# Attention in 64-key slots, twelve chunks instead of 22 tiles, in a fused attention and MoE kernel

## The chip, the cores and the metric

One Trainium2 chip, one of its cores. The metric is the device time of one execution in microseconds (us), the median of the runs shown; lower is better. The engines are called as in the profile: PE (TensorE matmul; PEld is its weight load), DVE (VectorE), ACT (ScalarE), POOL (GpSimd) and SP (SyncE, which here only issues DMAs).

## The reference

Strided and local attention over two batches, eight heads, 576 positions, then two expert layers over the 1152 tokens. Heads 0 to 3 see the 32 positions up to their own; heads 4 to 7 see the earlier positions of their own residue modulo 32.

```python
mask_local = (rel >= 0) & (rel < 32)
mask_strided = (rel >= 0) & (pos[None, :] % 32 == pos[:, None] % 32)
scores = np.where(masks, scale * q @ k.T, -1e9)
attn = softmax(scores)                      # the row maximum is taken off first
x = (attn @ v)                              # (1152, 512)
x = ((x @ w1) * (x @ w2)) @ w3 @ w_out      # 512 -> 1024 -> 1024 -> 512
out = sum(p[:, e:e+1] * (np.maximum(x @ e1[e], 0) @ e2[e]) for e in range(4))
```

The scale of q and k makes the scores large, so the softmax needs its maxima.

## The kernel before

The program is written in the order in which each engine shall run its instructions (`tc.manual_schedule`), and each engine runs its own list strictly in that order. It has three parts: attention; the gated product `ab = (x w1) * (x w2)`; and what follows (x3, and the experts in products with split operands).

**Attention** runs in tiles. A tile of the local heads (g = 0) holds 96 queries and up to 128 keys of four heads; a tile of the strided heads (g = 1) holds six or seven residues of 18 positions, 108 or 126 queries against as many keys. A batch has six local and five strided tiles, so there are 22. A tile goes through these methods (class `Tile`): `scores` (L281: one bf16 product of an identity with the mask, then four f32 products, all into one PSUM bank), `maxima` (L291, DVE), `exps` (L298, ACT, four instructions with their sums), `normalise` (L306, DVE), `transposes` (L314, PE), `evac` (L321, half on ACT, half on DVE), `pv` (L325, PE), `put` and `put_lo` (L334, L347: the result split into x_hi on ACT and x_lo on DVE). The loop at L645 is a software pipeline over steps s: in step s the scores of tile s, the normalisation of tile s - 1, the transposes of tile s - 3 and the value products of tile s - 4 are issued.

**Loads.** `load_group` (L241) loads q, k and v of a batch and a group on the SP queue: k as tk, q as two tiles tq with one head of a pair each, the other half zero. All four groups are issued ahead of the loop. q and k of one group are 1.18 MB (576 KB and twice 288 KB). The program gives its DMAs eight semaphores in turn (DMAHW0 to 7), so a DMA waits until the one eight places before has landed.

**Weights.** Class `Chunk` (L109) makes two f32 parts out of a 1 MB load of 64-bit numbers in steps: `round_up` and `magnitude` on ACT, `clamp` (L132), `shift` (L135), `sign` (L138), `add` (L142) on DVE, `split_hi` on ACT, `split_lo` (L159) on DVE. `advance()` (L222) issues the next step, four steps per chunk. There are two raw buffers, so `add` of chunk c is what frees the buffer for the load of chunk c + 2, and `load_next` (L177) issues that load on SP just there.

**The ab units.** `run_unit` (L629) issues one unit of `ab_block` (L353): 24 products of 288 columns, with two steps of the weights. A unit needs x_hi and x_lo of its whole batch and the chunk w12[ft]; two units use one chunk. The loop starts units at step 15 (L644), when all eleven tiles of batch 0 are through, and one unit is issued per step.

Of the kernel before, what the change touches and what calls it, by code (L numbers as in the profile page):

```python
# [18 lines left out]
P = 128  # L19
W = 32  # L20
# [3 lines left out]
RS = [(0, 7), (7, 7), (14, 6), (20, 6), (26, 6)]  # L24
HB = S // 2
# [15 lines left out]
def kernel(  # L41
# [36 lines left out]
    ident_b = const.tile([P, P], BF16, name="ident_b")  # L78
    m_loc = const.tile([P, P], BF16, name="m_loc")
    m_str = const.tile([P, 7, NB], BF16, name="m_str")  # L80

    def constants():
        make_identity(nc, ident_b)
        nc.gpsimd.memset(m_loc, 0.0)

        nc.gpsimd.affine_select(out=m_loc, in_=m_loc, compare_op=ALU.is_ge, fill=NEG,
                                base=W, pattern=[[-1, P]], channel_multiplier=1)
        nc.gpsimd.affine_select(out=m_loc, in_=m_loc, compare_op=ALU.is_ge, fill=NEG,
                                base=-1, pattern=[[1, P]], channel_multiplier=-1)
        make_identity(nc, ident)  # L90
        nc.gpsimd.memset(m_str, 0.0)

        nc.gpsimd.affine_select(out=m_str, in_=m_str, compare_op=ALU.is_ge, fill=NEG,
                                base=0, pattern=[[-NB, 7], [-1, NB]], channel_multiplier=1)
        nc.gpsimd.affine_select(out=m_str, in_=m_str, compare_op=ALU.is_ge, fill=NEG,
                                base=NB - 1, pattern=[[NB, 7], [0, NB]], channel_multiplier=-1)

    def warm_up():

        idle = tmp.tile([P, P], F32, tag="pT", name="idle")  # L100
        nc.vector.memset(idle, 0.0)
# [70 lines left out]
    live = 8  # L172
# [66 lines left out]
    qkv = {}  # L239

    def load_group(b, g, zeros, cut=0):  # L241
# [7 lines left out]
        for c in ([slice(0, cut), slice(cut, S)] if cut else [slice(0, S)]):  # L249
            pairs = slice(2 * g, 2 * g + 2)  # L250
            nc.sync.dma_start(out=tk[:, :, c], in_=kT[b, pairs, :, c].rearrange("k p n -> p k n"))
            for j, r in enumerate(rows):
                queue = nc.scalar if cut and j and c.start == 0 else nc.sync
                queue.dma_start(out=tq[j][r, :, c], in_=qT[b, pairs, r, c].rearrange("k p n -> p k n"))
        vs = []
        src, n = ((v_loc, NL), (v_str, len(RS)))[g]
        for k in range(2):
            tv = wp.tile([P, n, P], F32, tag="w", name="tv")
            nc.sync.dma_start(out=tv, in_=src[b, k])
            vs.append(tv)  # L260
        qkv[b, g] = (tq, tk, vs)

    class Tile:


        def __init__(self, index, b, g, t):
            self.index, self.b, self.g, self.t = index, b, g, t
            self.last = t == (NL, len(RS))[g] - 1
            if g == 0:
                self.nq = QL  # L270
                self.q0 = QL * t
                self.k0 = max(QL * t - W, 0)
                self.nk = QL * (t + 1) - self.k0
                self.mask = m_loc[:QL, P - self.nk:]
            else:
                r0, nr = RS[t]
                self.nq = self.nk = nr * NB
                self.q0 = self.k0 = r0 * NB
                self.mask = flat(m_str)[:self.nq, :self.nk]

        def scores(self):  # L281
            tq, tk, _ = qkv[self.b, self.g]
            nq, nk = self.nq, self.nk
            self.sc = ps_sc.tile([P, 4, P], F32, tag="sc", name="sc")
            mm(self.sc[:nq, :, :nk], ident_b[:nq, :nq], self.mask.unsqueeze(1).to_broadcast([nq, 4, nk]),
               start=True, stop=False)
            for h in range(4):
                mm(self.sc[:nq, h, :nk], tq[h % 2][:, h // 2, self.q0:self.q0 + nq],
                   tk[:, h // 2, self.k0:self.k0 + nk], start=False, stop=h == 3)

        def maxima(self):  # L291
            nq, nk = self.nq, self.nk
            self.neg = small.tile([P, 4], F32, tag="neg", name="neg")
            nc.vector.tensor_reduce(out=self.neg[:nq], in_=self.sc[:nq, :, :nk], axis=mybir.AxisListType.X,
                                    op=ALU.max, negate=True)
            nc.vector.tensor_scalar_mul(self.neg[:nq], self.neg[:nq], SCALE)  # L296

        def exps(self):  # L298
            nq, nk = self.nq, self.nk
            self.p = p_ring[self.index % 4]  # L300
            self.sum = small.tile([P, 4], F32, tag="sum", name="sum")
            for h in range(4):
                nc.scalar.activation(self.p[:nq, h, :nk], self.sc[:nq, h, :nk], AF.Exp,  # L303
                                     bias=self.neg[:nq, h:h + 1], scale=SCALE, accum_out=self.sum[:nq, h:h + 1])

        def normalise(self):  # L306
            nq, nk = self.nq, self.nk
            rec = small.tile([P, 4], F32, tag="rec", name="rec")
# [520 lines left out]
```

## Time and profile before

| | us |
|---|---|
| runs shown | 647.49 (646.29 to 649.39), three runs |
| the profiled execution, its own time | 648.42 |
| its span in the profile | 646.6 |
| PE busy in the span | 629.1 (97%) |
| DVE busy | 470.6 (73%) |
| ACT busy | 291.7 (45%) |

The profiled execution is 0.93 us above the median of the runs, and 1.8 us lie around its span. PE busy counts a pipelined product to its modelled end, so 97% does not say that PE is at its peak. The first two or three slices of 16 us each are the attention; from there on the profile's row of PE stands at nine tenths or more.

### The profile page before, as it was taken

Reading aid. Unit: us, or ns where it says so; the run is one execution under the profiler, and the core shown is the slowest. Engines: PE = TensorE matmul, PEld = TensorE weight load, DVE = VectorE, ACT = ScalarE, POOL = GpSimd, SP = SyncE. Lnnn points to the kernel's source line nnn. Section 1 sums busy time; section 2 is a strip of 40 time slices with the busy share of each in tenths; the row PEclk is TensorE's granted clock in tenths of the full one; section 3 lists DMA queues with packets and bytes.
Section 4 is the critical chain, followed back from the end, with each engine's and each line's share of the span. In section 5 each row is a group of like instructions: output and inputs, shape, how many; then the busy total and the mean of one; then the engine's idle time right before and its main releaser. Section 6 shows DMA issues by size and latency. Waiting matters only on the chain.

```text
span 646.6 us, 10360 instructions
## 1 busy us (share of the span) xinstructions
PE 629.1 (97%) x4052; PEld 572.7 (89%) x4052; DVE 470.6 (73%) x888; ACT 291.7 (45%) x628; POOL 6.9 (1%) x18
## 2 busy tenths in 40 slices
PE   7769999999999999999999999999999999999998
PEld 6659989999888999988999889988788989899896
DVE  8899999599875423777887787787776566665743
ACT  6787776466554323343333343344433333333321
POOL 4000000000000000000000000000000000000000
PEclk9989999999999999999999999999999999999999
DMA  8943133134433310234353355334478474656311
GB/s 227 308 133 131 66 131 131 67 131 143 183 131 130 131 66 1 67 131 188 137 188 138 134 192 183 142 131 163 163 260 322 151 247 153 228 177 239 130 66 66
DMA packets 26385, 98.73 MB, mean 153 GB/s; under 512 B 2528, under 2 KB 3808, under 8 KB 23776
## 3 DMA queue, kind: packets, MB, share of 16 engines
q1 hardware_dynamic: 26192, 97.97, 43.5%
q8 instruction: 32, 0.52, 0.4%
q14 instruction: 17, 0.14, 0.1%
q10 hardware_dynamic: 144, 0.10, 0.1%
HBM read 78.92 MB, written 19.14 MB: 152 GB/s over the span
## 4 chain that ended last, share of the span: by engine, by line
PE 85%; DVE 8%; DMA 3%; ACT 2%; SPq 1%; issue 1%; DVEq 0%
PE g_acc L233 10%; PE g_acc L234 10%; PE g_acc L232 10%; PE ab_acc L232 5%; PE ab_acc L234 4%; PE ab_acc L233 4%; PE m_a L232 4%; PE m_a L234 4%; PE m_a L233 4%; PE x_acc L232 3%; PE x_acc L233 3%; PE x_acc L234 3%; PE m_b L234 3%; PE m_c L232 3%; PE m_c L233 3%; PE m_c L234 3%
## 5 line engine op out<-in xcount | busy, mean ns | idle before, releaser
L517 ACT ACTIVATE h_hi<-u 128x320 fp32r<-128x320 f32 (+1 forms) x128 | 56.9, 445 | 189.2 <-DVE u L523 189.2
L233 PE MATMUL g_acc<-w_lo,h_hi 128*128 128x512 f32 (+1 forms) x296 | 114.9, 388 | 0.0
L232 PE MATMUL g_acc<-w_hi,h_hi 128*128 128x512 f32 (+1 forms) x296 | 114.7, 387 | 0.0
L234 PE MATMUL g_acc<-w_hi,h_lo 128*128 128x512 f32 (+1 forms) x296 | 114.6, 387 | 0.0
L523 DVE TENSOR_TENSOR u<-m_b,u 128x320 f32<-128x320 f32 (+1 forms) x96 | 40.8, 453 | 54.4 <-PE m_b L234 54.4
L456 DVE TENSOR_TENSOR w_lo<-raw,w_hi 128x768 fp32r<-128x768 f32 x64 | 69.4, 1085 | 12.0 <-ACT w_hi L454 11.9
L232 PE MATMUL ab_acc<-x_hi,w_hi 128*128 128x288 f32 x256 | 76.5, 299 | 0.0
L234 PE MATMUL ab_acc<-x_hi,w_lo 128*128 128x288 f32 x256 | 75.4, 295 | 0.0
L233 PE MATMUL ab_acc<-x_lo,w_hi 128*128 128x288 f32 x256 | 75.4, 294 | 0.0
L234 PEld LDWEIGHTS g_acc<-w_hi,h_lo 128*128 128x128 f32 x296 | 55.6, 188 | 12.2
L232 PEld LDWEIGHTS g_acc<-w_hi,h_hi 128*128 128x128 f32 x296 | 55.8, 189 | 8.6
L233 PEld LDWEIGHTS g_acc<-w_lo,h_hi 128*128 128x128 f32 x296 | 55.6, 188 | 8.4
L519 DVE SCALAR_TENSOR_TENSOR h_lo<-u,h_hi 128x320 fp32r<-128x320 f32 (+1 forms) x128 | 57.7, 451 | 3.5 <-ACT h_hi L517 1.4
L454 ACT CAST w_hi<-raw 128x768 fp32r<-128x768 f32 x64 | 59.9, 936 | 0.0
L232 PEld LDWEIGHTS ab_acc<-x_hi,w_hi 128*128 128x128 f32 x256 | 48.0, 187 | 1.5 <-issue 0.3
L233 PEld LDWEIGHTS ab_acc<-x_lo,w_hi 128*128 128x128 f32 x256 | 48.0, 188 | 0.0
L234 PEld LDWEIGHTS ab_acc<-x_hi,w_lo 128*128 128x128 f32 x256 | 48.0, 188 | 0.0
L303 ACT ACTIVATE p_pair<-sc,neg 96x128 f32<-96x128 f32 (+3 forms) x88 | 30.4, 355 | 18.5 <-DVE neg L296 17.3
L233 PE MATMUL m_b<-b_t,s_hi 128*128 128x320 f32 (+1 forms) x128 | 37.8, 295 | 0.0
L523 DVE TENSOR_TENSOR u<-m_a,u 128x320 f32<-128x320 f32 (+1 forms) x64 | 28.9, 452 | 11.8 <-PE m_a L234 11.8
L456 DVE TENSOR_TENSOR s_lo<-raw,s_hi 128x1024 fp32r<-128x1024 f32 x16 | 19.6, 1225 | 23.2 <-ACT s_hi L454 23.2
L121 ACT ACTIVATE raw<-raw 128x1024 int32<-128x1024 uint32 x20 | 23.5, 1174 | 27.4 <-DMA raw<-in_w3T_dram 19.5
(145 smaller groups left out, 1479.4 us busy)
## 6 DMA issues: line engine op xcount, KB each, us to landing
raw<-in_e_dram SPq DMA_DIRECT2D x32, 1024.0 KB, 5.2
raw<-in_w_dram SPq DMA_DIRECT2D x8, 1024.0 KB, 4.9
raw<-in_w3T_dram SPq DMA_DIRECT2D x8, 1024.0 KB, 4.8
stored<-s_hi SPq DMA_DIRECT2D x16, 512.0 KB, 2.6
stored<-s_lo SPq DMA_DIRECT2D x16, 512.0 KB, 2.6
s_hi<-stored SPq DMA_DIRECT2D x16, 512.0 KB, 4.7
s_lo<-stored SPq DMA_DIRECT2D x16, 512.0 KB, 6.2
raw<-in_w_out_dram SPq DMA_DIRECT2D x4, 1024.0 KB, 4.8
```

What stands on the lines that cost most here:

```text
L121: nc.scalar.activation(self.low, self.low.bitcast(U32), AF.Copy, scale=2.0 ** -29)
L232: mm(acc, lh, rh, start=first, stop=False)
L233: mm(acc, lh, rl, start=False, stop=False)
L234: mm(acc, ll, rh, start=False, stop=last)
L303: nc.scalar.activation(self.p[:nq, h, :nk], self.sc[:nq, h, :nk], AF.Exp, bias=self.neg[:nq, h:h + 1], scale=SCALE, accum_out=self.sum[:nq ...
L454: nc.scalar.copy(dst[0], src)
L456: nc.vector.tensor_tensor(out=dst[1], in0=src, in1=dst[0].bitcast(F32), op=ALU.subtract)
L517: nc.scalar.activation(hi, src, AF.Relu)
L519: nc.vector.scalar_tensor_tensor(out=lo, in0=src, scalar=0.0, in1=hi.bitcast(F32), op0=ALU.max, op1=ALU.subtract)
L523: nc.vector.tensor_tensor(out=out, in0=acc, in1=b, op=ALU.add)
```

## The change

The change rewrites the attention (class `Chunk4` for `Tile`), its loads, its place in the loop and the constants.

- A chunk has slots of 64 key columns. Local: six blocks of 32 queries, each against its own 32 keys and the 32 before; the four heads lie in four 32-partition groups of the PSUM bank. So a local chunk has 24 products of 32 queries by 64 keys. Strided: slots of 54 (three residues of 18), two heads side by side in partition halves; 16 products. Six local and six strided chunks, twelve in all.
- The maximum is subtracted on DVE from PSUM into SBUF, the exponential is one ACT instruction in place, the sum is a DVE reduction.
- A chunk is transposed in three (local) or four (strided) products of 128 by 128, evacuated by ACT alone, and multiplied with v in 24 or 16 products of 64 or 54 rows, into two banks.
- The loop has a step less of depth: the transposes come two steps behind the scores and the value products three.
- Loads: the first piece of q and k holds 288 positions (before 192); the value loads are cut up (393 KB per local chunk in one to three DMAs, 0.58 MB for the strided heads of a batch in six); q, k and v of the strided heads of batch 1 are issued after step 7. The second q tile of batch 0 goes by the ACT queue.
- Weight steps: none before step 5, three each in steps 5 to 8 (before: one each in steps 6 to 14). From step 9 on, two units and four weight steps per step.
- Products of zeros without use (`keep_warm`): 14 at the start as before, then 6, 4, 4 and 4 behind the scores of chunks 0 to 3.

```diff
+CUT = 288
...
+        def scores(self):
+            tq, tk = qk[self.b, self.g]
+            bank = ps_sc.tile([P, 512], F32, tag="sc", name="sc")
...
+                mm(self.sc, flat(i_loc), mask, start=True, stop=False)
+                for s, i in enumerate(self.blocks):
+                    k0 = max(i - 1, 0) * W
+                    for h in range(4):
+                        mm(self.sc[32 * h:32 * h + 32, s], tq[h % 2][:, h // 2, W * i:W * i + W],
+                           tk[:, h // 2, k0:k0 + 2 * W], start=False, stop=s == 5)
...
+        def maxima(self):
+            nc.vector.tensor_reduce(out=mx[:, :s], in_=self.sc, axis=mybir.AxisListType.X, op=ALU.max)
+            self.frame = p_ring[self.index % 4]
+            self.p = self.frame[:, :s, :self.nk]
+            nc.vector.tensor_tensor(out=self.p, in0=self.sc, in1=self.wide(mx), op=ALU.subtract)
...
+        def exps(self):
+            nc.scalar.activation(self.p, self.p, AF.Exp, scale=SCALE)
+
+        def sums(self):
...
+            nc.vector.tensor_reduce(out=rec, in_=self.p, axis=mybir.AxisListType.X, op=ALU.add)
+            nc.vector.tensor_scalar_add(rec, rec, 1e-9)
+            nc.vector.reciprocal(rec, rec)
...
+        keep_warm = warm_up()
+        load_qk(0, 0, nc.vector, CUT)
+        local_masks()
...
+        load_v_loc(0, 0)
+        load_qk(0, 1, nc.gpsimd)
+        strided_masks()
+        load_v_loc(0, 1)
+        load_v_loc(0, 2)
+        load_v_str(0)
         load_next()
         load_next()
+        load_qk(1, 0, nc.gpsimd)
+        for c in range(3):
+            load_v_loc(1, c)
...
+        for s in range(n + 3):
             if s < n:
+                chunks[s].scores()
+                chunks[s].maxima()
+                chunks[s].exps()
+                keep_warm({0: 6, 1: 4, 2: 4, 3: 4}.get(s, 0))
             if 1 <= s <= n:
+                chunks[s - 1].sums()
+                chunks[s - 1].normalise()
+            if 2 <= s < n + 2:
+                chunks[s - 2].transposes()
+                chunks[s - 2].evac(nc.scalar.copy)
+            if 3 <= s:
+                c = chunks[s - 3]
+                c.pv()
+                c.put()
+                c.put_lo()
...
+            if s > 8:
                 run_unit()
+                run_unit()
+            elif s > 4:
+                advance(3)
+            if s == 7:
+                load_qk(1, 1, nc.gpsimd)
+                load_v_str(1)
```

Two places in the lists of instructions matter below. The first is SP's list. In the kernel before, the last loads ahead of the loop are q and k of the two groups of batch 1 (tk_205 and tk_217 with their tq) and their v; the third and fourth weight loads (raw64_546, raw64_691), which wait for DVE's `add`, come behind them:

```order
L254 DMA tq_204<-in_qT_dram 64x2x576 [waits DMAHW1_49]
L259 DMA tv_211<-in_v_loc_dram 128x768 [waits DMAHW2_49]
L259 DMA tv_213<-in_v_loc_dram 128x768 [waits DMAHW3_49]
L251 DMA tk_217<-in_kT_dram 128x2x576 [waits DMAHW4_49]
L254 DMA tq_215<-in_qT_dram 64x2x576 [waits DMAHW5_49]
L254 DMA tq_216<-in_qT_dram 64x2x576 [waits DMAHW6_49]
L259 DMA tv_223<-in_v_str_dram 128x640 [waits DMAHW7_49]
L259 DMA tv_225<-in_v_str_dram 128x640 [waits DMAHW0_49]
L117 DMA raw64_546<-in_w12_dram 128x2048 [waits DMAHW1_49,DVE_49,Activation_49]
L117 DMA raw64_691<-in_w12_dram 128x2048 [waits DMAHW2_49,DVE_49,Activation_49]
```

In the change the third and fourth weight loads (raw64_639, raw64_716) come first, and q and k of the strided heads of batch 1 (tk_720, tq_718, tq_719) stand behind the fourth:

```order
L277 DMA tv_loc_239<-in_v_loc_dram 64x2x256 [waits DMAHW0_49]
L277 DMA tv_loc_239<-in_v_loc_dram 64x2x384 [waits DMAHW1_49]
L132 DMA raw64_639<-in_w12_dram 128x2048 [waits DMAHW2_49,DVE_49,Activation_49]
L132 DMA raw64_716<-in_w12_dram 128x2048 [waits DMAHW3_49,DVE_49,Activation_49]
L266 DMA tk_720<-in_kT_dram 128x2x576 [waits DMAHW4_49]
L269 DMA tq_718<-in_qT_dram 64x2x576 [waits DMAHW5_49]
L269 DMA tq_719<-in_qT_dram 64x2x576 [waits DMAHW6_49]
L298 DMA tv_str_726<-in_v_str_dram 54x2x512 [waits DMAHW7_49]
```

What moved: the last q and k went from ahead of the third weight load to behind the fourth, which waits for DVE's `add` of chunk w12[1].

The second place is PE's list at its first ab product (L232 before, L247 in the change). Before, ahead of it stand scores, transposes and value products of tiles whose q and k came with the loads ahead of the loop:

```order
L285 MATMUL sc<-m_loc,ident_b 96x512
L288 MATMUL sc<-tk,tq 96x128 x4
L318 MATMUL tp<-ident,p_pair 128x96 [waits PE_49]
L318 MATMUL tp<-ident,p_pair 128x96 x3
L331 MATMUL o<-pT,tv 64x96 [waits DMAHW2_49,Activation_49]
L331 MATMUL o<-pT,tv 64x96
L331 MATMUL o<-pT,tv 64x96 [waits DMAHW3_49,DVE_49]
L331 MATMUL o<-pT,tv 64x96
L232 MATMUL ab_acc<-x_hi,w_hi 128x288 [waits PE_49]
```

In the change, ahead of the first ab product stand the scores of chunk 9, the first of the strided heads of batch 1, and they wait for the DMAs of that group (semaphores 4, 5 and 6 of the list above):

```order
L338 MATMUL sc<-m_str,i_str 128x432
L344 MATMUL sc<-tk,tq 54x54 [waits DMAHW5_49,DMAHW4_49,Pool_49]
L344 MATMUL sc<-tk,tq 54x54 [waits DMAHW6_49,Pool_49]
L344 MATMUL sc<-tk,tq 54x54 x14
L375 MATMUL tp<-ident,p_pair 128x128 [waits DVE_49,PE_49]
L375 MATMUL tp<-ident,p_pair 128x128 x2
L392 MATMUL o<-pT,tv_loc 64x32 [waits DMAHW3_49,Activation_49]
L392 MATMUL o<-pT,tv_loc 64x32
L392 MATMUL o<-pT,tv_loc 64x32 [waits PE_49]
L392 MATMUL o<-pT,tv_loc 64x32 x21
L247 MATMUL ab_acc<-x_hi,w_hi 128x288 [waits DVE_49,PE_49]
```

What moved: a wait for a load stands in front of the first ab product, where before only value loads (the waits of the L331 rows) had one.

## Rows read from the trace of the kernel before

**Rows 1.** Busy time by stretch (us of the stretch, then each engine), attention, mix, ab alone.
```profile
48.50:97.70 49.20, 48.65 (x414) 45.47 (x410) 47.64 (x101) 36.73 (x110) 0.00 (x0) 1.00 0.31 108
110.00:120.00 10.00, 10.00 (x78) 10.00 (x77) 6.37 (x14) 4.39 (x8) 0.00 (x0) 1.00 0.43 160
```

**Rows 2.** Timeline of PE: start us, duration us, line, count; first ab product, last attention.
```profile
48.57 0.40 PE L232 MATMUL ab_acc<-x_hi,w_hi 128*128 128x288 f32 x1
...
97.24 0.59 PE L331 MATMUL o<-pT,tv 108*64 108x108 f32 x8
97.76 0.40 PE L232 MATMUL ab_acc<-x_hi,w_hi 128*128 128x288 f32 x1
```

**Rows 3.** DVE's groups by shape up to 48.3 us: count, busy us, mean ns.
```profile
L312 DVE TENSOR_TENSOR p_pair<-p_pair,rec 108x432 f32<-108x432 f32 x3 | 1.8, 608 | 0.1
L294 DVE TENSOR_REDUCE neg<-sc 108x4 f32<-108x432 f32 x3 | 1.8, 601 | 0.0
L312 DVE TENSOR_TENSOR p_pair<-p_pair,rec 96x384 f32<-96x384 f32 x2 | 1.1, 554 | 0.1
L294 DVE TENSOR_REDUCE neg<-sc 96x4 f32<-96x384 f32 x2 | 1.1, 550 | 0.1
L310 DVE RECIPROCAL rec<-rec 96x4 f32<-96x4 f32 x9 | 1.6, 174 | 0.3
L348 DVE TENSOR_TENSOR x_lo<-o,x_hi 128x192 fp32r<-128x192 f32 x6 | 2.1, 346 | 0.0
L348 DVE TENSOR_TENSOR x_lo<-o,x_hi 128x216 fp32r<-128x216 f32 x3 | 1.6, 537 | 0.0
```

**Rows 4.** The same view, the weight steps.
```profile
L138 DVE SCALAR_TENSOR_TENSOR t<-raw,t 128x1024 int32<-128x1024 int32 x2 | 2.4, 1214 | 0.0
L132 DVE TENSOR_SCALAR t<-t 128x1024 f32<-128x1024 f32 x2 | 1.4, 690 | 0.0
L135 DVE TENSOR_SCALAR t<-t 128x1024 int32<-128x1024 int32 x2 | 1.4, 684 | 0.0
L127 DVE TENSOR_SCALAR t<-raw 128x1024 int32<-128x1024 int32 x1 | 0.7, 694 | 0.5 <-DMA raw<-in_w_dram 0.5
L142 DVE CUSTOM_DVE_ANT_0 t<-raw,t 128x2048 uint16<-128x2048 uint16 x1 | 1.2, 1221 | 0.0
L159 DVE TENSOR_TENSOR w_lo<-t,w_hi 128x1024 fp32r<-128x1024 f32 x1 | 1.2, 1217 | 0.0
```

**Rows 5.** Timeline of PE at its first scores and at tile 6: waits for q, in brackets.
```profile
5.39 0.89 PE L288 MATMUL sc<-tk,tq 128*96 128x96 f32 x8 [1.02 <-DMA tq<-in_qT_dram]
...
17.91 0.92 PE L288 MATMUL sc<-tk,tq 128*126 128x126 f32 x6 [0.71 <-DMA tq<-in_qT_dram]
```

**Rows 6.** Busy time by stretch; the last two columns are DMA share and GB/s.
```profile
0.00:10.00 10.00, 7.51 (x48) 5.75 (x49) 7.15 (x13) 4.26 (x18) 6.92 (x18) 1.00 0.76 216
10.00:20.00 10.00, 7.88 (x74) 6.34 (x73) 8.74 (x29) 7.82 (x40) 0.00 (x0) 1.00 1.05 304
20.00:30.00 10.00, 7.97 (x80) 6.34 (x78) 9.19 (x27) 8.01 (x39) 0.00 (x0) 1.00 1.04 283
```

**Rows 7.** DMA issues between 49 and 56 us (one load, nothing beside it): us to landing.
```profile
raw<-in_w_dram SPq DMA_DIRECT2D x1, 1024.0 KB, 4.8
```

**Rows 8.** The SP queue's own waits up to 60 us: total us, times, longest us.
```profile
SPq L117 <- DVE t L142: 29.9, 3, 14.0
```

**Rows 9.** Timeline of PE: eight passes each over 96 columns, scores, transposes, value products.
```profile
30.83 0.84 PE L288 MATMUL sc<-tk,tq 128*96 128x96 f32 x8
...
31.51 0.54 PE L318 MATMUL tp<-ident,p_pair 108*108 108x108 f32 x4
```

**Rows 10.** The same, value products of a local tile, in two column halves.
```profile
19.10 0.55 PE L331 MATMUL o<-pT,tv 128*64 128x96 f32 x8
```

**Rows 11.** Busy time by stretch around a gap of PE; the column after POOL is PE's granted clock.
```profile
42.30:44.40 2.10, 0.19 (x4) 0.00 (x0) 2.00 (x8) 1.24 (x7) 0.00 (x0) 1.00 0.00 0
44.40:48.50 4.10, 4.03 (x25) 3.25 (x25) 4.00 (x11) 3.59 (x14) 0.00 (x0) 0.58 0.00 0
```

More of the change, by code (lines that the diff above doesn't have):

```diff
@@ L103, in warm_up, with keep_warm @@
         zeros = idle.bitcast(BF16)
-        acc = bank("idle")
-        for i in range(WARM):
-            mm(acc[:, :2 * P], zeros[:, :P], zeros, start=i == 0, stop=i == WARM - 1)
+        def keep_warm(n):
+            if n:
+                acc = bank("idle")
+            for i in range(n):
+                mm(acc[:, :2 * P], zeros[:, :P], zeros, start=i == 0, stop=i == n - 1)
+        keep_warm(WARM)
+        return keep_warm
     class Chunk:
@@ L252, in load_group @@
             for j, r in enumerate(rows):
-                queue = nc.scalar if cut and j and c.start == 0 else nc.sync
+                queue = nc.scalar if b == 0 and j else nc.sync
                 queue.dma_start(out=tq[j][r, :, c], in_=qT[b, pairs, r, c].rearrange("k p n -> p k n"))
-        vs = []
-        src, n = ((v_loc, NL), (v_str, len(RS)))[g]
-        for k in range(2):
-            tv = wp.tile([P, n, P], F32, tag="w", name="tv")
-            nc.sync.dma_start(out=tv, in_=src[b, k])
-            vs.append(tv)
@@ new lines, in load_qk, with load_v_loc, load @@
+        qk[b, g] = (tq, tk)
+    def load_v_loc(b, c):
+        tv = wp.tile([P, 2, 3, P], F32, tag="w", name="tv_loc")
+        def load(dst, rows, t0, n):
+            nc.sync.dma_start(out=dst, in_=v_loc[b, :, rows, t0:t0 + n].rearrange("k p t d -> p k t d"))
+        lower, upper, middle = slice(0, 64), slice(64, P), slice(W, 3 * W)
+        if c == 0:
+            load(tv[lower, :, 0:1], lower, 0, 1)
+            load(tv[upper, :, 0:1], middle, 0, 1)
+            load(tv[:, :, 1:], slice(0, P), 1, 2)
+        elif c == 1:
+            load(tv, slice(0, P), 3, 3)
+        else:
+            load(tv[lower, :, 0:1], lower, 0, 1)
+            load(tv[lower, :, 1:], middle, 1, 2)
+            load(tv[upper], middle, 3, 3)
+        vals[b, 0, c] = tv
@@ new lines, in load_v_str @@
+    def load_v_str(b):
+        threes = [wp.tile([P, n, P], F32, tag="w", name="tv_str") for n in (8, 4)]
+        for k in range(2):
+            rows = slice(64 * k, 64 * k + T3)
+            for tv, t0, n in ((threes[0], 0, 4), (threes[1], 4, 1)):
+                nc.sync.dma_start(out=tv[rows, :2 * n].rearrange("p (h t) d -> p h t d", h=2),
+                                in_=v_str[b, k, :2 * T3, t0:t0 + n].rearrange("(h p) t d -> p h t d", h=2))
+            nc.sync.dma_start(out=threes[1][64 * k:64 * k + NB, 2:], in_=v_str[b, k, 2 * T3:2 * T3 + NB, :2])
+        vals[b, 1] = threes
@@ L347, in put_lo @@
         def put_lo(self):
-            nc.vector.tensor_tensor(out=self.x[1], in0=self.o, in1=self.x[0].bitcast(F32), op=ALU.subtract)
+            for o, (hi, lo) in self.ends:
+                nc.vector.tensor_tensor(out=lo, in0=o, in1=hi.bitcast(F32), op=ALU.subtract)
     ab_hi, ab_lo = {}, {}
```

229 lines of the change are left out of this document (114 added, 115 removed).

## The prediction

> **What bounds the kernel now.** I read the busy time by stretch first. From 48.5 us on PE is full: 48.65 of 49.20 us while attention and ab units alternate, then 10.00 of 10.00 [rows 1]. So the end moves with two numbers: the moment T0 at which the ab products can start, and the attention work R that PE still has to do after T0. Whatever is done earlier than T0 on any engine counts only through T0.
>
> The timeline of PE gives both for the kernel before: the first ab product starts at 48.57, the first one behind the last attention product at 97.76 [rows 2]. Ten units lie between. A unit is 24 products, and 78 run in 10 us [rows 1], so it takes 3.08 us and ten take 30.8. R is 97.76 - 48.57 - 30.8 = 18.4, and T0 + R = 67.0 us. The change is a gain if its T0 + R is below that.
>
> DVE is the other full engine: 47.64 of 49.20 us [rows 1]. It sets T0, since x_lo of batch 0 comes last from it, and its list is in order.
>
> **The change: DVE's work up to T0.** Durations by shape are in [rows 3]. A local chunk has 384 columns: its maximum takes 0.55; the subtraction is not in the trace and is priced as L312 on 384 columns, 0.55 (between 0.35, a 192-column pass, and 0.7, twice that); the sum as L294, 0.55; two small ones 0.17 each; the scaling 0.55. That is 1.10 + 1.43. Its two x_lo passes of 192 columns are 0.69. A strided chunk has 432 columns: 1.21 + 1.54, and x_lo passes with scattered writes, from L348 on 216 columns (0.54): 1.1 for the chunks with two such, about 1.4 for the one with four halves.
>
> When x of batch 0 is ready (step 8), DVE has done nine maxima (six local, three strided: 10.2 us), eight normalisations (11.8), the x_lo of six chunks (5.7) and nine weight steps: one L127, two L132, two L135, two L138, two L142, one L159, 9.5 us [rows 4]. Together 37.2 us. The exponentials go from four ACT instructions per tile to one per chunk; ACT had room, so I cost that at nothing, with DVE as its cover.
>
> DVE starts when the first scores are there. Before, the q for them came at 5.39 [rows 5]; the first pieces are now 576 KB instead of 384, at 216 GB/s [rows 6] up to 0.9 us more. I take 5.9, plus 1.3 for mask and scores: 7.2. Without waits x would be ready at 44.4.
>
> **Two waits for loads.** q and k of the strided heads of batch 0 came at 17.91 [rows 5], behind 3.15 MB; now it is 2.75 MB. In proportion that is 15.6; at the stretches' full rates (216, then 304 GB/s [rows 6]) 11.9. I take 14.5. DVE gets there at 7.2 + three maxima + two normalisations = 13.4, and scores cost 2 us, so it waits some 2.5 us. q and k of batch 1's local heads stand behind 7.4 MB: at the rates of [rows 6] 27.8, in proportion 32; I take 29.5. DVE gets there near 28.6 (16.5 plus three maxima, three normalisations, the x_lo of chunks 0 to 2 and three weight steps), and the scores are done at 30.8: another 2.2. So x is ready at 49.1, no earlier than before, though DVE has less to do.
>
> **The wait that the change adds.** The load of q and k for chunk 9 stands on SP behind the fourth weight load, and that one waits for `add` of w12[1], the last weight step of step 7. SP's waits for DVE's L142 are real waits here: 29.9 us in three [rows 8]. This `add` ends one maximum, one normalisation and one put (3.6 us) ahead of 49.1: at 45.5. Then 0.4 for the issue, 4.8 until the weight load has landed [rows 7], and 1.18 MB behind it in the same queue: 3.9 at 304 GB/s, 5.5 at 216 [rows 6]; I take 4.4. So chunk 9 has its q and k at 55.1. On PE its scores stand in front of the transposes of chunk 7, the products of chunk 6 and the first ab unit, all of which could have run.
>
> **PE's small products.** Eight f32 passes of 96 columns on the whole array take 0.84 [rows 9], while eight in two column halves take 0.55 [rows 10]: halves run side by side, some 0.11 to 0.14 per pair. A strided chunk has 16 such pairs with 54 columns: between 1.0 (0.06 each, by columns) and 2.1; I take 1.6, with the mask 2.0. Four column groups side by side are not in the trace. A local chunk has twelve rounds of four: 1.0 if they overlap as the halves do, 48 passes of 0.08, 3.8, if not at all. I take 1.0, and for the value products 1.0 (local) and 0.8 (strided), bounds 0.5 and 2.6 to 3.8 likewise. Transposes cost 0.13 each [rows 9].
>
> So behind 55.1 come 2.0 + 0.45 + 1.0 = 3.5 us. PE will then have stood for about ten microseconds. Before, a stretch of 2.1 us with 0.19 busy was followed by 4.1 us at a granted clock of 0.58, mostly the lower level, 1.2 GHz [rows 11]. I add 1.5. T0 is 60.1. The useless products run in steps 0 to 3, far ahead of this gap, and sit in waits for loads: nothing.
>
> **R after T0.** Scores of two chunks 4.0, transposes of four 2.2, value products of five 4.4: 10.6. DVE must keep pace: in steps 9 to 14 it has 24 weight steps (six chunks of 5.0 us by [rows 4], 30), 24 passes of 288 columns (some 0.45 each, 10.8) and 15.4 of attention, 56 us by summed durations, where PE has 37 + 10.6 = 47.6. Its records overlap a little, and it was nearly full before without stopping PE [rows 1]; I add 1.5 (between 0 and 8). T0 + R = 72.2.
>
> **The sum.** 72.2 - 67.0 = +5.2 us on the profiled execution's own 648.42 (span 646.6), so 653.6; the median of the runs lies 0.93 lower: 652.7. Nothing behind the 16 units of batch 0 changes.
>
> **A rule against the change.** The value loads of the strided heads now fill 54 partitions, before 128. The Trainium skill, "DMA: Bandwidth & Descriptors", section "Why a DMA increments its semaphore by 16 and not by 1", says that a DMA uses the largest number of engines up to 16 that divides its outermost dimension, so nine for 54. No run here shows it yet.
>
> **The rivals.**
> - *Held by nothing* (faster). If chunk 9's q and k land before x is ready, T0 is 49.1 and scores, transposes and products ahead of the first unit are hidden: R = 10.6 + 1.5, T0 + R = 61.2, -5.8, 641.7. For: the last `add` and DVE's put are only 3.6 us apart and all else in step 9 is ready. Against: it takes a landing by about 46, that is an `add` near 36.5, and DVE's work alone puts it at 40.8. Chance 0.17, mostly for errors in DVE's prices.
> - *No waits for the early loads* (no change). The loads stand in order of use; if both waits vanish, all is 4.7 earlier: 648.0. Chance 0.22.
> - *Slow value loads.* If loads into 54 partitions get nine sixteenths of the rate, the 0.58 MB of batch 0's strided values take 3.6 us instead of the 2.0 at 283 GB/s [rows 6], and the loads behind them, q and k of chunk 6 among them, come 1.6 later: 654.3. This is the rule above. Chance 0.06.
> - *Small products one after another.* A local chunk then costs PE 0.4 + 3.8 + 0.45 + 3.8 = 8.4 and a strided one about 6.3; PE, not DVE, is late at step 8, and R grows too: some 25 us, 675. Against: [rows 10]. Chance 0.07.
>
> **How the numbers follow.** My case has 0.48, its own range 649 to 659. A measurement here can tell 0.5%, 3.2 us, from no change. Slower: 0.44 of my case and the last two, 0.57. No change: 0.04 of my case and the second, 0.26. Faster: 0.17. The range 643.5 to 662 takes in my case, the second, the third and the near half of the first; the far half and the serial case, some 0.17, are left out.
>
> **What would show it.** In the profile after: x_lo of chunk 5 near 49; SP waiting for L157 ahead of the fourth weight load until about 45; PE idle before L344 of chunk 9 until about 55, released by a DMA of tq; the first ab product near 60; a fall of the granted clock there. If L344 at chunk 9 shows no wait, my main term is wrong; if DVE is ready with chunk 5 by 42, its prices are. If L334 takes over 2 us per chunk, the overlap is.

## The result and the profile after

The changed kernel takes 656.35 us (median of 4 runs, 654.76 to 656.45) where the kernel before, run beside it, takes 647.57: a ratio of 1.0128, interval 1.0099 to 1.0157. It is slower by 1.3%. The profiled execution took 656.45 us, its span is 654.6.

PE's timeline of the changed kernel (start, duration, line, form, count, the wait ahead of it in brackets), chunk 6 to the first ab products:

```profile
32.80 0.39 PE L334 MATMUL sc<-tk,tq 128*32 128x64 f32 x2 [5.65 <-DMA tq<-in_qT_dram]
34.13 1.50 PE L334 MATMUL sc<-tk,tq 128*32 128x64 f32 x46 [0.94 <-DMA tq<-in_qT_dram]
...
41.17 0.88 PE L334 MATMUL sc<-tk,tq 128*32 128x64 f32 x48
...
58.58 0.40 PE L344 MATMUL sc<-tk,tq 128*54 128x54 f32 x2 [11.87 <-DMA tq<-in_qT_dram]
59.74 1.71 PE L344 MATMUL sc<-tk,tq 128*54 128x54 f32 x30 [0.76 <-DMA tq<-in_qT_dram]
61.38 0.90 PE L375 MATMUL tp<-ident,p_pair 128*128 128x128 f32 x3
62.21 1.51 PE L392 MATMUL o<-pT,tv_loc 64*64 64x32 f32 x48
63.65 0.61 PE L247 MATMUL ab_acc<-x_hi,w_hi 128*128 128x288 f32 x1
...
107.61 0.40 PE L247 MATMUL ab_acc<-x_hi,w_hi 128*128 128x288 f32 x1
```

The first ab product starts at 63.65, where it started at 48.57 [rows 2]; ahead of it stand 12.6 us of waits for chunk 9's q. The first one behind the last attention product starts at 107.61 (97.76 before). As before, ten units of ab lie between the two, 30.8 us. So R, the attention work that PE still does after T0, is 107.61 - 63.65 - 30.8 = 13.2, and T0 + R is 76.8 where it was 67.0.

The SP queue's issues tell why chunk 9 is late (start, duration from the first to the last of a row):

```profile
41.96 8.71 SPq L132 DMA_DIRECT2D raw<-in_w_dram  x2
50.72 0.43 SPq L266 DMA_DIRECT2D tk<-in_kT_dram  x1
51.20 1.26 SPq L269 DMA_DIRECT2D tq<-in_qT_dram  x2
```

The row of L132 holds the third and the fourth weight load, issued at 41.96 and 50.32. SP's waits up to 60 us (us in total, times, longest), and DVE's timeline around them: first maximum of chunk 6, `add` of w12[1], x_lo of chunk 5.

```profile
SPq L132 <- DVE t L157: 25.0, 3, 8.6
```

```profile
35.68 0.56 DVE L350 TENSOR_REDUCE mx<-sc 128x6 f32<-128x384 f32 x1 [5.40 <-PE sc L334]
...
49.03 1.22 DVE L157 CUSTOM_DVE_ANT_0 t<-raw,t 128x2048 uint16<-128x2048 uint16 x1
...
52.72 0.85 DVE L432 TENSOR_TENSOR x_lo<-o,x_hi 128x108 fp32r<-128x108 f32 x4
```

The fourth weight load went out behind `add` of w12[1], which ran from 49.03 to 50.25, and q and k behind it. They were used from 59.74, and x of batch 0 had been ready at 53.57. Busy time by stretch (columns as in [rows 1], the third number from the end is the granted clock):

```profile
10.00:20.00 10.00, 7.65 (x204) 5.87 (x192) 8.40 (x21) 2.89 (x7) 1.86 (x2) 1.00 0.96 225
20.00:30.00 10.00, 5.43 (x136) 4.06 (x134) 8.00 (x19) 3.98 (x9) 0.00 (x0) 0.81 1.00 313
...
50.00:60.00 10.00, 0.66 (x8) 0.55 (x10) 6.98 (x15) 3.47 (x8) 0.00 (x0) 0.50 0.79 247
60.00:70.00 10.00, 10.00 (x117) 9.51 (x115) 5.46 (x12) 4.21 (x8) 0.00 (x0) 0.64 0.43 139
...
100.00:110.00 10.00, 8.80 (x90) 8.09 (x89) 7.87 (x14) 5.69 (x10) 0.00 (x0) 1.00 0.38 143
```

From 10 to 20 us the loads moved 225 GB/s (304 before, [rows 6]) with a DMA share of 0.96 (1.05 before). PE idles from 46.7 to 58.6, the granted clock falls to 0.50, which is 1.2 GHz, and is 0.64 on average over the ten us in which ab begins. Between 100 and 110 us PE loses another 1.2 us (0.9 behind ACT, 0.25 behind DVE).

DVE's groups up to 54 us (count, busy us, mean ns, idle time ahead):

```profile
L353 DVE TENSOR_TENSOR p_pair<-sc,mx 128x384 f32<-128x384 f32 x6 | 3.3, 558 | 0.4
L350 DVE TENSOR_REDUCE mx<-sc 128x6 f32<-128x384 f32 x6 | 3.3, 554 | 10.9 <-PE sc L334 10.9
...
L432 DVE TENSOR_TENSOR x_lo<-o,x_hi 128x108 fp32r<-128x108 f32 x6 | 1.8, 351 | 0.0
```

### The profile page after: what moved, and what is told of

Its sections match the earlier page's. It is cut to its first block, busy times and chain, and to the rows that moved or that the text cites. A ratio compares the mean times of both kernels' runs of the same rounds, so it can differ in the third digit from the quotient of the medians.

```text
span 654.6 us, 11331 instructions
## 1 busy us (share of the span) xinstructions
PE 619.3 (95%) x4622; PEld 565.3 (86%) x4622; DVE 458.4 (70%) x836; ACT 265.4 (41%) x464; POOL 10.6 (2%) x25
## 4 chain that ended last, share of the span: by engine, by line
PE 83%; DMA 8%; DVE 5%; ACT 2%; SPq 1%; issue 1%; DVEq 0%; ACTq 0%
PE g_acc L247 10%; PE g_acc L248 10%; PE g_acc L249 10%; PE ab_acc L247 4%; PE ab_acc L248 4%; PE ab_acc L249 4%; PE m_a L247 4%; PE m_a L249 4%; PE m_a L248 4%; DMA tq<-in_qT_dram 3%; PE x_acc L247 3%; PE x_acc L248 3%; PE x_acc L249 3%; PE m_b L248 3%; PE m_c L247 3%; PE m_c L248 2%
## 5 line engine op out<-in xcount | busy, mean ns | idle before, releaser
L247 PE MATMUL g_acc<-w_hi,h_hi 128*128 128x512 f32 (+1 forms) x296 | 114.3, 386 | 0.0
L247 PE MATMUL ab_acc<-x_hi,w_hi 128*128 128x288 f32 x256 | 77.1, 301 | 1.6 <-ACT pT L380 0.9
L540 DVE TENSOR_TENSOR w_lo<-raw,w_hi 128x768 fp32r<-128x768 f32 x64 | 69.4, 1085 | 12.0 <-ACT w_hi L538 11.9
L249 PEld LDWEIGHTS g_acc<-w_hi,h_lo 128*128 128x128 f32 x296 | 55.6, 188 | 11.6
L247 PEld LDWEIGHTS g_acc<-w_hi,h_hi 128*128 128x128 f32 x296 | 55.8, 188 | 8.0
L247 PEld LDWEIGHTS ab_acc<-x_hi,w_hi 128*128 128x128 f32 x256 | 48.7, 190 | 2.6 <-ACT pT L380 1.2
L607 DVE TENSOR_TENSOR u<-m_a,u 128x320 f32<-128x320 f32 (+1 forms) x64 | 28.9, 452 | 11.6 <-PE m_a L249 11.6
L607 DVE TENSOR_TENSOR u<-m_c,u 128x320 f32<-128x320 f32 (+1 forms) x64 | 29.0, 453 | 4.6 <-PE m_c L249 4.0
```

The source lines that it names most:

```text
L247: mm(acc, lh, rh, start=first, stop=False)
L249: mm(acc, ll, rh, start=False, stop=last)
L540: nc.vector.tensor_tensor(out=dst[1], in0=src, in1=dst[0].bitcast(F32), op=ALU.subtract)
L607: nc.vector.tensor_tensor(out=out, in0=acc, in1=b, op=ALU.add)
```

## The experiments

T0 is the start of the first ab product; M is the start of the first ab product behind the last attention product (48.57 and 97.76 in the kernel before). Both come from one profiled execution each, the times are medians; the profiled execution of e3_q_first lies 3.4 us above its median, that of g1_round_late 1.25. Each ratio is to the kernel before, run beside that kernel (medians 647.28 to 647.73). Where a diff starts with names in brackets, the kernel has the edits of those kernels too.

| kernel | time, us | ratio to before, interval | T0 | M |
|---|---|---|---|---|
| the change | 656.35 | 1.0128, 1.0099 to 1.0157 | 63.65 | 107.61 |
| e1_early | 648.82 | 1.0025, 1.0010 to 1.0041 | 54.47 | 99.20 |
| e2_before_advance | 649.91 | 1.0054, 1.0036 to 1.0072 | 54.45 | 100.01 |
| e3_q_first | 653.47 | 1.0102, 1.0058 to 1.0145 | 63.59 | 108.19 |
| e5_gap_filled | 654.65 | 1.0122, 1.0094 to 1.0150 | 62.36 | 104.72 |
| e7_no_empty | 656.09 | 1.0128, 1.0108 to 1.0147 | 63.76 | 106.99 |
| f1_order | 650.29 | 1.0038, 1.0025 to 1.0050 | 53.58 | 101.75 |
| f2_add_early | 653.91 | 1.0093, 1.0073 to 1.0114 | 56.44 | 106.53 |
| f3_warm | 652.24 | 1.0064, 1.0043 to 1.0086 | 55.33 | 105.08 |
| v64 | 655.01 | 1.0112, 1.0086 to 1.0138 | 62.52 | 106.62 |
| g1_round_late | 645.67 | 0.9979, 0.9962 to 0.9995 | 56.22 | 98.88 |
| g2_both | 641.58 | 0.9905, 0.9887 to 0.9924 | 49.39 | 92.78 |
| w_warm_probe | 641.54 | 0.9913, 0.9895 to 0.9931 | 47.21 | 91.52 |

**The wait for chunk 9.** First the loads of chunk 9 are taken out from behind `add`.

```diff
         for c in range(3):
             load_v_loc(1, c)
+        load_qk(1, 1, nc.gpsimd)
+        load_v_str(1)
...
-            if s == 7:
-                load_qk(1, 1, nc.gpsimd)
-                load_v_str(1)
```

> Loads of chunk 9 (q, k and values of batch 1's strided heads) moved ahead of the loop, behind those of the local heads, as in the kernel before. Theory: the wait of PE for chunk 9's q and k, which stand on SP behind the fourth weight load and so behind add of w12[1], sets T0. Then the wait of 11.9 us at L344 goes, T0 falls from 63.6 to the end of x_lo of chunk 5 (53 to 54.5), DVE becomes the next limit in the ab steps, and the time is 647 to 651. Rival: DVE's summed work in the ab steps sets the end whenever PE starts; then T0 falls just as far but the first ab product behind the last attention product stays near 107, and the time is 654 to 656.

Measured: 648.82 us, 7.5 less. Chunk 9's scores no longer wait. PE's timeline:

```profile
46.63 1.74 PE L344 MATMUL sc<-tk,tq 128*54 128x54 f32 x32
...
54.47 0.61 PE L247 MATMUL ab_acc<-x_hi,w_hi 128*128 128x288 f32 x1
...
99.20 0.40 PE L247 MATMUL ab_acc<-x_hi,w_hi 128*128 128x288 f32 x1
```

T0 falls by 9.2 us and M by 8.4: the theory holds, the rival (M stays) is out. The second kernel leaves the loads in step 7 and only exchanges them with the weight steps of that step:

```diff
+            if s == 7:
+                load_qk(1, 1, nc.gpsimd)
+                load_v_str(1)
             if s > 8:
                 run_unit()
                 run_unit()
             elif s > 4:
                 advance(3)
-            if s == 7:
-                load_qk(1, 1, nc.gpsimd)
-                load_v_str(1)
```

> The same loads stay in step 7, but are issued ahead of step 7's three weight steps, so behind the third weight load and ahead of the fourth. Theory (the wait for add is what makes them late): issued right behind the third weight load at 42, they land at 42 + 4.8 + 4.4 = 51.2, ahead of x_lo of chunk 5; no wait at L344 of over 1 us, and the time within 1.5 us of the first experiment. Rival (what counts is their place in the DMA queue against all other loads): the wait at L344 falls by less than half, and the time stays above 652.

Measured: 649.91 us, 1.1 above the first, T0 the same to 0.02 us. q and k were issued from 41.5 on, right behind the third weight load, and were used from 50.62 (expected 51.2); PE waited 3.4 us there, more than the 1 expected, but ahead of x of batch 0. As in the change they stand right behind one weight load here; only the wait for `add` is gone. So it is this wait, not the place among the bytes, that costs.

**The clock and the empty products.**

```diff
+            if s == 9:
+                keep_warm(100)
             if s < n:
                 chunks[s].scores()
```

> 100 empty products ahead of chunk 9's scores fill PE's gap from 46.4 to about 57.5 (100 at 0.109 us, the pitch of the empty products at 10 us). Theory: the gap lets the granted clock fall to 0.50, and scores, transposes, value products and the first 15 ab products then run at half pace, some 3 us in all; filled, the clock is 1.00 from 59 on, T0 falls by 1.5 to 2 and the time is 652.5 to 654. Rival: DVE or the load sets the end, and PE at half clock is hidden; then the time is 656 to 657. If the empty products themselves run at half clock they end near 68 and the time is about 665.

Measured: 654.65 us. PE's timeline:

```profile
55.79 4.20 PE L118 MATMUL idle<-idle 128*128 128x256 bf16 x37
...
60.11 1.01 PE L344 MATMUL sc<-tk,tq 128*54 128x54 f32 x32
61.05 0.55 PE L375 MATMUL tp<-ident,p_pair 128*128 128x128 f32 x3
61.52 0.90 PE L392 MATMUL o<-pT,tv_loc 64*64 64x32 f32 x48
62.36 0.40 PE L247 MATMUL ab_acc<-x_hi,w_hi 128*128 128x288 f32 x1
```

From the scores to the first ab product it takes 2.25 us instead of 3.91, and R falls from 13.2 to 11.6: the clock's price at M is 3.3 us. Of that 0.4 was lost again, as the scores began 0.4 later (the load itself had been issued 0.6 later too). M is 2.9 lower, the profiled span only 1.75, since PE loses 1.45 us between 110 and 120, more than the change does there (0.4). T0 fell by 1.3, where the theory had 1.5 to 2, and the time lies between theory and rival. Its interval is almost the change's (the runs lie between 652.42 and 656.95), so the trace shows the clock's price and the runs don't show a gain. The change's own empty products are another matter:

```diff
-                keep_warm({0: 6, 1: 4, 2: 4, 3: 4}.get(s, 0))
```

> The changed kernel without the empty products of steps 0 to 3 (those of the warm-up stay). Theory: they lie in waits for loads, far ahead of T0, which the wait for chunk 9 sets; the time stays at 655.5 to 657.5 and T0 at 63 to 64.5, whatever the clock does before 20 us. Rival: without them the clock falls in the first waits, DVE gets its scores later (1 us per chunk at half clock), add of w12[1] and so everything is 2 to 4 us later: 658.5 to 661.

Measured: 656.09 us, T0 63.76. The clock from 10 to 20 us is 0.50 without them instead of 1.00, and nothing comes of it.

**The wait for chunk 6.**

```diff
+        load_qk(1, 0, nc.gpsimd)
         load_next()
         load_next()
-        load_qk(1, 0, nc.gpsimd)
```

> The first two weight loads are moved behind q and k of chunk 6. Theory: the 5.4 us for which DVE waits for chunk 6's scores come from the 2.1 MB of weights ahead of them. They then land near 28.5 instead of 34.1, DVE's wait for scores at L350 of chunk 6 falls under 1.5, it waits 1 to 2 for the first weight load instead, add of w12[1] ends near 46.5 instead of 50.25, and the time is 652 to 653.5. Rival: the wait has to do with small packets of the values that go on in the same engines, not with the order; then q and k come at 32 or later and the time is 655 to 656.5.

Measured: 653.47 us, but its runs lie between 649.74 and 656.85, its interval overlaps the change's, and the profiled run is the slowest; T0 there is 63.59. The median falls into the forecast, the mechanism does not: chunk 6's wait for scores did go, but DVE stood 6.3 us before the first weight load (1 to 2 expected), and chunk 9 was as late as ever. The two cures belong together, with weight steps that start when the weights are there:

```diff
 (e1_early and e3_q_first)
-            elif s > 4:
-                advance(3)
+            elif s > 5:
+                advance(4)
```

> The first experiment (loads of chunk 9 ahead of the loop), and q and k of chunk 6 ahead of the first two weight loads, with the twelve weight steps of steps 5 to 8 put into steps 6 to 8, four in each, so that DVE doesn't stand before the first weight load (it stood 6.3 us there with the order alone changed). Theory: with the wait at chunk 9 gone, T0 follows x_lo of chunk 5, and that follows chunk 6's q and k; they come near 31, so DVE goes on at 31.5 instead of 35.4, T0 is 49.5 to 51 instead of 54.5, and the time is 643.5 to 646. Rival: the DMA engines are full up to 35 whatever the order, chunk 6 comes no earlier than 33.5, the weights later, and the time stays at 647.5 to 650.

Measured: 650.29 us, 1.5 more than e1_early (1.0 if each is taken against the kernel before beside it), though DVE did go on at 31.22. The waits between 40 and 56 us (engine, tile, line, what it waited for: us in total, times, longest):

```profile
ACT raw L136 <- DMA raw<-in_w_dram: 6.1, 1, 6.1
PE tp L375 <- DVE p_pair L370: 6.0, 2, 4.6
DVE x_lo L432 <- ACT x_hi L428: 2.7, 1, 2.7
```

ACT's list is in order too. It stood at `round_up` of w12[2], whose load `add` had issued only at 43.1, and DVE waited behind it for x_hi. Neither theory nor rival had this: of the 4 us that DVE had gained 0.9 are left at T0, and M is 2.5 later than in e1_early.

**The weight loads.** The same wait shows behind T0 in e1_early, the waits from 54 to 125 us:

```profile
ACT raw L136 <- DMA raw<-in_w_dram: 14.7, 5, 3.3
ACT raw L136 <- DMA raw<-in_w_out_dram: 7.5, 2, 4.3
```

A load goes out at `add` of one chunk, and `round_up` comes three slots later. Moving `add` up to `sign` and `round_up` down to `magnitude` makes it five:

```diff
-            if after:
-                after.round_up()
             c.sign()
+            c.add()
             yield True
             if after:
+                after.round_up()
                 after.magnitude()
-            c.add()
             yield True
```

> As f1_order, and in the weight steps add comes one slot earlier (together with sign) and round_up one slot later (together with magnitude). Theory: behind T0 the ACT queue stands at L136 for weight loads (22 us in the first experiment, of which PE loses some 2) since a load is issued by add only 5 to 7 us ahead of its round_up; with five slots between them the waits of L136 fall below 8 us in all, PE is 9.8 or more of 10 from 80 us to 110 us, and the time falls by another 1 to 2 us. Rival: PE's idle time there is DVE's (work of 9.3 to 9.8 of 10 us), then PE's loss and the time stay within 0.7 us of f1_order.

Measured: 653.91 us, 3.6 worse. The waits for w12 are gone, but PE is at 7.8 to 8.4 of 10 from 60 to 90 us. It stands three times, 5.8 us in all, behind ACT's copy of the transposes, ACT behind DVE's subtraction, and DVE's `clamp`, ahead of that, behind ACT's magnitude (5.3 us in four). In this profiled execution chunk 6 also came later, its first maximum at 32.82 instead of 31.22. Both forecasts miss. Empty products on top, 20 each ahead of the scores of steps 7 to 9 (`keep_warm({7: 20, 8: 20, 9: 20}.get(s, 0))`):

> As f2_add_early, and 20 empty products ahead of the scores of steps 7, 8 and 9, where PE waits for DVE. Theory: the granted clock is then near 1.00 when the ab products begin, and the first three microseconds run at full instead of half pace: 1 to 1.5 us less than f2_add_early. Rival: PE is idle for so long between the steps that 20 products don't hold the clock; then it stays at 0.5 at T0 and the time is the same, or up to 2 us more, since the products stand in front of the scores.

Measured: 652.24 us, 1.7 less than f2_add_early. The clock is 0.99 from 40 to 50 us, but again 0.50 from 50 to 60, where the ab products begin: the time is the theory's, the clock at T0 the rival's. What gave the 1.7 us is open.

The other way to part the load from its use, on top of e1_early, leaves `add` alone and lets ACT round late:

```diff
+            c.round_up()
             if before:
                 before.split_lo()
             c.shift()
             yield True
-            if after:
-                after.round_up()
             c.sign()
```

> e1_early with one edit in the weight steps: round_up of a chunk (ACT, L136) moves from the sign step of the chunk before to the shift step of its own, so that ACT first touches a loaded chunk at its magnitude, four slots behind the load's issue, not three. Theory: what is left of the loss against the kernel before is PE standing behind ACT, which stands at L136 for weight loads (22 us from 54 to 125 us); these waits fall under 5 us, PE is over 9.8 of 10 from 80 to 110, and the time is 646 to 647.5. Rival: DVE's work is the limit there, or the wait only moves from L136 to the magnitude (L144); then 648.3 to 649.5.

Measured: 645.67 us, below the kernel before. Busy time by stretch, first e1_early, then g1_round_late:

```profile
80.00:90.00 10.00, 9.48 (x116) 8.85 (x118) 9.52 (x20) 6.53 (x15) 0.00 (x0) 1.00 0.37 116
90.00:100.00 10.00, 8.92 (x111) 8.11 (x103) 7.98 (x12) 6.02 (x11) 0.00 (x0) 1.00 0.37 129
100.00:110.00 10.00, 9.55 (x72) 9.35 (x72) 8.58 (x18) 4.98 (x11) 0.00 (x0) 1.00 0.46 174
```

```profile
80.00:90.00 10.00, 10.00 (x105) 9.77 (x104) 9.90 (x19) 6.93 (x14) 0.00 (x0) 1.00 0.30 107
90.00:100.00 10.00, 9.70 (x125) 9.13 (x124) 10.00 (x17) 8.71 (x18) 0.00 (x0) 1.00 0.52 168
100.00:110.00 10.00, 10.00 (x78) 10.00 (x77) 9.86 (x17) 6.76 (x12) 0.00 (x0) 1.00 0.42 151
```

PE loses 0.3 us there instead of 2.05 (it is at 9.70 of 10 in the second stretch, where the theory had over 9.8), and ACT's waits for weights from 54 to 125 us fall from 22.2 to 1.8. The mechanism came out as the theory had it, and so did the time, within 0.4. The two traces alone don't show 3 us: in this profiled execution chunk 6's q came 1.6 us later than in e1_early's, T0 is 1.75 later, M only 0.3 earlier, and the two profiled times are 0.96 apart. The medians, 3.15 apart, are of ten and seven runs. With the order of loads and fewer steps ahead of T0:

```diff
 (g1_round_late and e3_q_first)
-            elif s > 4:
+            elif s > 5:
                 advance(3)
```

> g1_round_late with f1_order's order of loads and nine weight steps in steps 6 to 8, three in each, instead of twelve. Theory: in f1_order DVE went on at 31.2 as expected, but lost it again at 44 to 52 behind ACT, which stood at L136 for the third weight load; without that stand x of batch 0 is ready at 48 to 49.5, T0 is below 50.5, and the time is 643.5 to 646. Rival: the weight steps left out ahead of T0 come back behind it, where DVE has no room; then T0 falls and the time is within 1 us of g1_round_late.

Measured: 641.58 us, 0.95% faster than the kernel before and 2.25% faster than the change, and 1.9 below the forecast's range; T0 is 49.39. x of batch 0 was ready at 47.8. Late rounding, order and fewer early steps came together here; which of them it takes for the 4.1 us below g1_round_late was not separated. PE's timeline shows who was last:

```profile
45.29 1.71 PE L342 MATMUL sc<-tk,tq 128*54 128x54 f32 x30 [0.88 <-DMA tq<-in_qT_dram]
47.15 0.87 PE L373 MATMUL tp<-ident,p_pair 128*128 128x128 f32 x3 [0.16 <-DVE p_pair L368]
47.95 1.51 PE L390 MATMUL o<-pT,tv_loc 64*64 64x32 f32 x48
49.39 0.61 PE L245 MATMUL ab_acc<-x_hi,w_hi 128*128 128x288 f32 x1
```

**The engines of a 54-partition load.** The values of the strided heads are laid out again among the inputs, so that each load fills 64 partitions:

```diff
-            rows = slice(64 * k, 64 * k + T3)
+            rows = slice(64 * k, 64 * k + 64)
...
-                                in_=v_str[b, k, :2 * T3, t0:t0 + n].rearrange("(h p) t d -> p h t d", h=2))
+                                in_=v_str[b, k, :P, t0:t0 + n].rearrange("(h p) t d -> p h t d", h=2))
```

> The changed kernel with the values of the strided heads laid out so that each load fills 64 partitions instead of 54 (the same runs of 2048 and 512 bytes, the same number of loads, 18% more bytes; the ten extra rows of each are not read). The rule of the Trainium skill, DMA: Bandwidth & Descriptors, section Why a DMA increments its semaphore by 16 and not by 1 (9 engines for 54 partitions, 16 for 64): q and k of chunk 6 come 1.5 to 2 us earlier, at 32.2 to 32.7 instead of the 33.9 to 34.2 of the runs so far, and the time falls by about that, to 654.5 to 655. Rival (all engines are busy with other loads then, and the rate is that of short runs): 33.8 to 34.4 and 656 to 657.

Measured: chunk 6's last q at 32.95, between the two forecasts; with the same order of loads up to there the change, e1, e2, e5 and e7 have it at 33.28 to 34.20, g1_round_late at 35.03. So one run lies 0.33 below the lowest of six that are 1.75 apart, and what the 54 partitions cost in this kernel is not shown. The time, 655.01, can't be told from the change's. So the last kernel measures it by itself, and tries the clock once more on g2_both:

```diff
+            keep_warm({8: 16, 9: 20}.get(s, 0))
             if s < n:
                 chunks[s].scores()
...
         load_probs()
+        probe = const.tile([P, 512], F32, name="probe")
+        for rows in 3 * (54, 64):
+            nc.sync.dma_start(out=probe[:rows], in_=v_str[0, 0, :rows, :4].rearrange("p t d -> p (t d)"))
```

> Two separate things on top of g2_both. (1) 16 and 20 empty products ahead of the scores of chunks 8 and 9. In g2_both PE runs at 1.2 GHz (granted clock 0.50) from 38 to 51 us, and the chain scores (1.71), transposes (0.87), value products (1.50) of step 9 ends last ahead of T0, 1.6 us behind x. Theory: at full clock the chain takes 2.3 instead of 4.1, T0 falls from 49.4 to 47.8 to 48.3, the first ab products run at full pace, and the time falls by 1.5 to 2.5, to 639 to 640. Rival: from 40 us on DVE is full (9.7 to 9.9 of 10 us), so PE ends earlier but waits for DVE: within 0.7 us of g2_both. (2) In a stretch in which SP has nothing to do, behind the load of the probabilities, six loads of 2048 bytes per partition into a tile that nothing reads, of 54 and 64 partitions in turn, each waiting for the one before. Rule of 9 engines for 54 partitions: the packets of a load of 54 take about 6 in a row on each engine (first start to last end over 0.65 times ... of one packet's time times 6), those of 64 about 4, so 54 takes longer than 64 although it moves less. Rival: the same engines for both; then 54 takes no longer than 64.

Measured, the loads: the DMA view of the window of the second load of 54 (117 to 118 us) and of that of 64 (119.5 to 120.35): packets by size, then packets, MB and the share of 16 engines in the window.

```profile
DMA packets 63, 0.11 MB, mean 111 GB/s; under 512 B 9, under 2 KB 9, under 8 KB 63
q1 hardware_dynamic: 63, 0.11, 33.8%
...
DMA packets 80, 0.13 MB, mean 154 GB/s; under 512 B 16, under 2 KB 16, under 8 KB 80
q1 hardware_dynamic: 80, 0.13, 53.5%
```

From the first packet's start to the last one's end the three loads of 54 took 0.77, 0.84 and 0.97 us, those of 64 took 0.61, 0.73 and 0.75; 5.9 to 6.4 data packets were under way at a time, and 9.5 to 11.1. A load of 54 moves 0.69 of the bytes per time (0.111 MB in 0.86 us, 0.131 in 0.70). Besides its 54 or 64 packets of 2048 bytes it has 9 or 16 small ones. The Trainium skill, "DMA: Bandwidth & Descriptors", section "Why a DMA increments its semaphore by 16 and not by 1", says that a load runs on the largest number of engines up to 16 that divides its outermost dimension, and that each engine in use ends with a write to the semaphore. That is nine engines for 54 partitions and sixteen for 64, and the nine and sixteen small packets agree. With nothing else to do the price is 0.69 of the rate, less than the nine sixteenths of the rival.

Measured, the clock: 641.54 us, the same as g2_both. The clock was 1.00 from 40 us on and T0 fell by 2.2 to 47.21, but R rose from 12.6 to 13.5. PE's timeline shows where it gave that part back:

```profile
47.21 0.40 PE L245 MATMUL ab_acc<-x_hi,w_hi 128*128 128x288 f32 x1
...
53.15 0.40 PE L245 MATMUL ab_acc<-x_hi,w_hi 128*128 128x288 f32 x1 [2.18 <-ACT pT L378]
```

ACT had stood 3.5 us for a weight load until 50.32, and then for DVE's subtraction, which ended at 52.14. So PE does wait for others, as the rival had it, though for both ACT and DVE. The profiled execution still keeps 1.3 us at M and 1.0 of its span; the medians, of six runs between 640.20 and 643.88 and four between 639.83 and 642.57, don't show it.

## Why the prediction was right, and where it was off

The sign and the mechanism were right: chunk 9's q and k wait for `add`, and PE and everything queued on it wait for them. Forecast was 652.7; measured 656.35, 3.7 more, inside the case's own range of 649 to 659. Part of that closeness is luck: T0 + R was off by 4.6, and 2.5 us came back in a stage that the forecast held to be unchanged. By its steps:

- **DVE's prices** held: 0.55 to 0.56 for each local pass, the subtraction among them, 0.35 per scattered x_lo pass of 108 columns. From chunk 6's first maximum (35.68) to x ready (53.57) it took 17.9 us; the step had 18.3 (30.8 to 49.1), its own terms 18.8.
- **Chunk 3's q** was used from 14.94 (taken: 14.5). The step's sum is 0.6 short here: 14.5 and 2.0 for the scores, less 13.4, is a wait of 3.1, not 2.5. Measured, DVE stood 0.4: the scores took 1.0, and DVE came later, having stood 1.2 for chunk 1.
- **Chunk 6's q and k** are the mis-sized term: 34.13 measured, 29.5 taken, outside the step's 27.8 to 32, and DVE stood 5.4 us for the scores where 2.2 were taken. No row shown gives the 32: in proportion to the 17.91 us for 3.15 MB, as for chunk 3, 7.4 MB take 42. And the rates of the kernel before don't hold stretch by stretch. Of the 3.0 MB that it moved from 10 to 20 us 1.25 were weights, in packets of 8192 bytes; in the change the weights come from 20 to 30, and it moves 225 and then 313 where there were 304 and then 283. In the first 30 us together it moved 7.3 MB instead of 8.0. Some of that may lie in the runs of 512 to 2048 bytes of the new value loads (before: 2560 and 3072): by the mean times of the packets, an estimate, the 1.77 MB of values ahead of chunk 6 took 8.1 us of all 16 engines, and would have taken 6.9 in the old runs. The rest is open.
- **`add` of w12[1]** ended at 50.25 (45.5), later by what chunk 6 was late; from there to q's landing it took 9.5 us (9.6).
- **The clock** cost 3.3 us at M (e5), half of it ahead of T0 and half behind; 1.5 was taken, all ahead of T0. From the landing to T0 it took 3.9 us (5.0). R was 13.2 (12.1): besides the clock's 1.6 it holds the 1.2 that PE stood between 100 and 104 us, most of it behind ACT, where the step had 1.5 for DVE.
- **PE's small products** were cheap as taken: 48 score passes of a local chunk in 0.88 us at full clock, a strided chunk 1.0 (1.6 taken). "Small products one after another" is out.
- **"Nothing behind batch 0's units changes"** was wrong in both directions. PE lost 0.6 us more from M to the last ab product; and from the start of the first expert product to the start of the last, the changed kernel needs 378.4 us where the kernel before needs 380.9, for the same 2232 products. Every version of the study has this 378.4. 0.65 us of it is one wait for a load at 480 us, the rest about a nanosecond per product. No run explains it.

T0 + R rose by 9.8 instead of 5.2 (T0 was forecast 3.55 too low, R 1.1); with the 0.6 lost and the 2.5 won later the profiled time rose by some 8.0.

Of the rivals, "held by nothing" is what g2_both is, once the loads stand ahead of the loop, chunk 6 comes earlier and ACT does not stand at the weights: T0 49.39 and M 92.78 against its 49.1 and 92.0. That the time, 641.58 us, meets its 641.7 as well is luck: M fell by 5.0 instead of 5.8, and the 2.5 us of the expert stage, which the rival did not have, came on top. "No waits for early loads" and "slow value loads" were each wrong as cases; of the second the mechanism shows in the loads by themselves (w_warm_probe), but a price in this kernel does not (v64). What made the change slow is the place of one group's loads: without it 7.5 of the 8.8 us are gone (7.2 with each kernel against the one before beside it). Whether the late rounding would help the kernel before as well was not tried.

## What to carry to other kernels

When a change moves a load behind one that waits for a compute step, follow the whole chain (DVE step, SP wait, the transfers, PE's in-order list) and price the time until that step from the arrival of its own inputs. Curing one wait of an in-order engine may pay nothing as long as the next one in line stays: on top of e1_early the order of loads gave nothing, the late rounding 3 us, and both together, with fewer weight steps ahead of T0, 7. A gap of PE cost twice here, once idle and once at half clock behind it; filling it won 2.9 us (e5) and 1.3 us (w_warm_probe) at M, but nothing that the times of the runs show, and PE stood behind ACT and DVE instead.

## What was not expected of the hardware

- Four column groups of 32 run side by side almost fully: 48 f32 passes of 64 columns take 0.88 us at full clock, where eight of 96 columns on the whole array take 0.84 [rows 9]; that is 768 columns for each group and 768 for the array.
- The DMA engines were nearly as full at 225 GB/s as at 304. Runs of 512 bytes took 0.042 us each, runs of 8192 bytes, the weights, 0.37 us (the change's packet records up to 36 us, means), so a byte in the short run cost almost twice as much. The old value loads lie between: 0.18 us for 2560 and for 3072 bytes.
- A gap of PE is paid twice: behind the 11.9 us without work the scores of chunk 9 took 1.71 us at 1.2 GHz where 1.01 does at 2.4 (e5), and the granted clock was back at 1.00 only within the first unit: 0.50 from 64 to 66 us, 0.69 from 66 to 68, 1.00 behind.
